# Attention beside a long convolution on one core: score tiles taken three in a row, probability products by halves of the queries

## The chip, the cores and the metric

The program runs on one core of one Trainium2 chip. The metric is device time in microseconds (us) of one execution: 1081.78 us is the median of three runs of the kernel before (1081.75 to 1082.9). A profiled execution of the same program is the source of every other number ahead of the prediction.

Four engines matter. TensorE (PE) does all matrix products and writes them to PSUM; a load of its stationary operand is shown apart as PEld. ScalarE (ACT) does almost nothing but the exponentials. VectorE (DVE) copies results out of PSUM and does the elementwise work. GpSimd (POOL) and SyncE (SP) mostly issue DMA transfers. Each engine runs its own instructions strictly in the order in which the program wrote them, and waits on semaphores for the others.

## The reference

Two independent results are computed and put side by side. Left, multi-query attention with 32 heads of width 16 and one shared key and value:

```python
q = (x @ wq).reshape(B, S, H, Dh)        # S = 2048, D = 512, H = 32, Dh = 16
k = x @ wk;  v = x @ wv                  # one head of keys and values for all
scores = einsum("bhqd,bkd->bhqk", q, k) * Dh ** -0.5
p = softmax(scores, axis=-1)
a = einsum("bhqk,bkd->bhqd", p, v).reshape(B, S, H * Dh) @ wo
```

Right, a gated long convolution per channel:

```python
k_shift = causal depthwise conv of k with 4 taps
kv = k_shift * v
y = causal conv of kv with ssm_k (length 2048, by FFT) + kv * ssm_D
b = q * y
out = concatenate([a, b], axis=-1)
```

## The kernel before, in words

**Attention, the main line.** The queries are cut into 32 blocks of four heads by 512 positions (`NQ` = 32), the keys into 16 tiles of 128 (`NKT` = 16). That gives 512 steps `i`, with n = i // 16 the query block and k = i % 16 the key tile. A step has two tiles of scores, so there are 1024 tiles `u`, two heads each. `scores(u)` puts two matmuls side by side in the upper and the lower half of the array (L673) into one of three PSUM tiles of two banks, and has ACT write exp of it (L681) into an SBUF tile `p` of 128 x 1024 floats, one of `PB` = 5. `pv(i)` multiplies the two `p` tiles of step i with the values (L690): four matmuls of 32 output columns, one for each head, side by side in the array, which add up over the 16 key tiles in one PSUM bank, `self.acc`. After the last key tile DVE copies that bank out (L700, tile `ao`) and DMA takes it to DRAM.

The order of the main line is written by hand in `attend`: in step i the score tiles 2i+4 and 2i+5, then `pv(i)`, then one call of `fill.step(i)`.

**Everything else is fill.** Query projections (`rest_of_q`), the normalization of finished heads (`wo_heads`), the output projection (`wo_part`), and the convolution by a two-stage Fourier transform (`conv_pe` for its matrix products and transposes, `conv_dve` for its elementwise stages) are Python generators. Each yields the price of its next piece, for PE and for DVE, before it writes it. `_Fill.step` adds `RATE` = 480 for PE and 1450 for DVE to two credits at each step and takes the next pieces from the generators in their order while the credit lasts, at most one piece with a PE price. The transposes of the convolution (`turn`, L248) and `bound`, one small matmul for each projection chunk (L555), have prices of their own. A piece of the helper `mm` (L191) is four matmuls side by side; a PE piece of price 920 is one `mm` of 512 columns or two of 256. HOLD keeps a PSUM bank with one generator over several steps. `finish` writes what is left of all generators ahead of the very last `pv`.

**PSUM.** Three score tiles take six banks. The other two (pool `pf`) serve `self.acc` and the fill: while the sum of a query block runs, one bank is left for the fill.

**The end.** `wo_part` has rows of `wo_rows` for head groups 12 and 13 (copied out at L786), then `over` (L818 to L824: transposes, reciprocal and product on DVE, for two halves of the last block but one), then eight products that are added to `wp` at L806 and L811; `last` does the last query block.

**Places of the text.** Lines here are those of the kernel before; the changed program numbers the same lines a little higher (scores L698, probability products L718, `mm` L196).

Of the kernel before, what the change touches and what calls it, by code (L numbers as in the profile page):

```python
# [19 lines left out]
P = 128  # L20
# [6 lines left out]
CB = 256  # L27
# [11 lines left out]
PB = 5  # L39


RATE = 480.0, 1450.0
MOST = 1400.0, 2900.0
SLACK = 60.0
OB = 5

Q_AT = 0, 40, 170, 295
# [37 lines left out]
class _Emit:  # L85
# [107 lines left out]
    def forward(self, src, c, m, ft):  # L193

        b = self.bank()
        for q in range(2):  # L196
            self.mm(b[:, q * CB : (q + 1) * CB], ft[:, q, :], src)
        self.nc.vector.tensor_copy(c[:, :, m, :], b.rearrange("p (q n) -> p q n", q=2))  # L198
# [36 lines left out]
    def long_forward(self, blk, hin, ch):  # L235
# [19 lines left out]
        for m in range(0, 16, 2):  # L255
            if m < 12:
                ft[m // 2 + 2] = self.table("ff", m // 2 + 2)
                yield 500, 700
                turn(m + 4)
            for i in range(2):  # L260
                yield 920, 700
                self.forward(hT[m][:, i, :], ch, m + i, ft[m // 2][:, i])
# [22 lines left out]
    def short_forward(self, blk, tpb, kk, cx):  # L285
# [3 lines left out]
        kv, ft = {}, {i: self.table("ff", i) for i in range(2)}  # L289

        def prod(m2):
# [3 lines left out]
            v = w.tile([P, 2, CB], F32, tag="s2", bufs=S2, name=self.nm("v"))  # L295
            nc.gpsimd.dma_start(v, self.vr[:, r, cs])
            if 2 <= m2 + 1 < 8:
                ft[m2 + 1] = self.table("ff", m2 + 1)
            a = w.tile([P, 2, CB], F32, tag="s2", bufs=S2, name=self.nm("a"))
# [4 lines left out]
            for i in (2, 1, 0):  # L304
                t = w.tile([P, 2, CB], F32, tag="s2", bufs=S2, name=self.nm("t"))
# [6 lines left out]
            kv[m2] = a  # L312

        yield WAIT, 3
        yield from prod(0)
        for m2 in range(8):
            if m2 < 7:
                yield from prod(m2 + 1)
            for i in range(2):
                yield 920, 700  # L320
                self.forward(kv[m2][:, i, :], cx, 2 * m2 + i, ft[m2][:, i])
# [16 lines left out]
    def backward(self, blk, cx, places):  # L338
# [15 lines left out]
        for m2 in range(8):  # L354
            if m2 < 6:
                load(m2 + 2)
            r = self.s2("r")
            for i in range(2):
                m = 2 * m2 + i
                yield 920, 450  # L360
                b = self.bank()
                for cc in range(2):
                    self.mm(
                        b[:, 0:CB],
# [5 lines left out]
                nc.vector.tensor_tensor(r[:, i, :], b[:, 0:CB], q[m2][:, i, :], ALU.mult)  # L370
# [5 lines left out]
    def conv_pe(self):  # L376

        yield from self.conv_load()
        self.sp = {}
        ld = self.short_load(0)  # L380
        yield WAIT, 5
        yield from self.short(0, ld)
# [6 lines left out]
        ld = self.short_load(1)  # L389
        yield from self.after(("y", 0))  # L390
        yield from self.backward(0, *self.sp["y", 0])
        yield from self.short(1, ld)
# [3 lines left out]
    def short(self, blk, loads):  # L396
        cx = self.spectrum()
        yield from self.short_forward(blk, *loads, cx)
        self.sp["cx", blk] = cx
        self.seen.add(("cx", blk))  # L400

# [132 lines left out]
    def q_mm(self, g, c, b, dk):  # L534
        self.mm(b, self.wq[g][:, dk, :], self.xT[c][:, dk, :], start=dk == 0, stop=dk == 3)
# [34 lines left out]
    def prologue(self):  # L570
# [5 lines left out]
        self.qa, self.st, self.pt = {}, {}, {}  # L576
# [42 lines left out]
        self.scores(3)  # L619

    def rest_of_q(self):
        for c, first in enumerate(Q_AT):
            while self.step < first:
                yield WAIT, 1
            for g in range(4):
                if c == g == 0:
                    continue
                if c or g > 1:
                    b = None
                    for dk in range(4):  # L630
                        yield (920, 0, HOLD) if dk < 3 else (920, 2600)
                        b = b or self.bank()
                        self.q_mm(g, c, b, dk)
# [5 lines left out]
            if c < 2:  # L639
                self.xT[c + 2] = self.w.tile([P, 4, 512], F32, tag="xt", bufs=2, name=f"xT{c + 2}")  # L640
                self.nc.sync.dma_start(self.xT[c + 2], self.xd[c])
        self.flag()

    def stack(self, n, rows=KR):

        c, h = n // 8, 4 * (n % 8)
        t = self.w.tile([P, 2, 512], F16, tag="st", bufs=3, name=self.nm("st"))
# [36 lines left out]
    def pv(self, i):  # L684
        nc, w = self.nc, self.w
        n, k = i // NKT, i % NKT
        if k == 0:
            self.acc = self.bank()
        for j in range(4):
            nc.tensor.matmul(  # L690
                self.acc[32 * j : 32 * j + 32, :],
                self.vx[:, k, :],
                self.pt[2 * i + j // 2][:, j % 2, :],
                start=k == 0,
                stop=k == NKT - 1,
            )
        if k < NKT - 1 or n == NQ - 1:
            return  # L698
        a = w.tile([P, 512], F32, tag="ao", bufs=2, name=self.nm("ao"))
# [6 lines left out]
    def attend(self, fill):  # L706
        self.od = self.dr.tile([NQ, P, 512], F32, name="od")
        for i in range(NQ * NKT):
            n, k = i // NKT, i % NKT
            self.step = i  # L710
            if k == 4 and 2 <= n + 1 < NQ:
                self.stack(n + 1)
            self.scores(2 * i + 4)
            self.scores(2 * i + 5)
            if i == NQ * NKT - 1:
                fill.finish()
            self.pv(i)
            fill.step(i)  # L718
# [42 lines left out]
    def wo_rows(self, i, groups):  # L761

        for G in groups:
            yield (920, 700) if G == groups[-1] else (920, 0, HOLD)
            if G == groups[0]:
                b = self.bank()
            self.mm(b, self.oc[G][:, i * P : (i + 1) * P], self.wo[G % 4], start=G == groups[0], stop=G == groups[-1])
# [80 lines left out]
class _Fill:  # L848
# [3 lines left out]
    def __init__(self, threads):  # L852
# [18 lines left out]
    def step(self, i):  # L871
# [3 lines left out]
        while more:  # L875
            more = False
            for t in self.threads:
# [3 lines left out]
                if a[0] > 0:  # L881
                    if c[0] < a[0] - SLACK or not once or self.holder not in (None, t):
# [14 lines left out]
    def finish(self):  # L897
        while any(t[0] is not None for t in self.threads):
            for t in self.threads:
                if t[0] is not None and next(t[0], None) is None:  # L900
                    t[0] = None
# [152 lines left out]
```

## Time and profile before

| | |
|---|---|
| median of the runs | 1081.78 us |
| the profiled execution, its own time | 1082.38 us |
| its span in the profile | 1080.5 us |
| granted TensorE clock over the span | 0.996 |
| PE busy | 1039.7 us, 96% |
| ACT busy | 976.5 us, 90%; 1024 exponentials |
| DVE busy | 612.1 us, 57% |
| POOL busy | 95.8 us, 9% |

A row of the page or of a group reads: line, engine, operation, output tile <- input tiles, shapes, xcount, then the busy time of the group and the mean of one in ns, then the idle time of the engine just ahead of the group and what ended it. A row of the timeline reads: start, length, engine, line, operation, xcount of instructions merged into the row, and in brackets the idle time before it with what ended it. Matmuls of four-byte floats are recorded as two instructions each, so a `pv` of four matmuls is a row of x8. Matmul records overlap; the distance between the starts of two rows is the better measure of what PE spends.

### The profile page before, as it was taken

Reading aid. Unit: us, or ns where it says so; the run is one execution under the profiler, and the core shown is the slowest. Engines: PE = TensorE matmul, PEld = TensorE weight load, DVE = VectorE, ACT = ScalarE, POOL = GpSimd, SP = SyncE. Lnnn points to the kernel's source line nnn. Section 1 sums busy time; section 2 is a strip of 40 time slices with the busy share of each in tenths; the row PEclk is TensorE's granted clock in tenths of the full one; section 3 lists DMA queues with packets and bytes.
Section 4 is the critical chain, followed back from the end, with each engine's and each line's share of the span. In section 5 each row is a group of like instructions: output and inputs, shape, how many; then the busy total and the mean of one; then the engine's idle time right before and its main releaser. Section 6 shows DMA issues by size and latency. Waiting matters only on the chain.

```text
span 1080.5 us, 21752 instructions
## 1 busy us (share of the span) xinstructions
PE 1039.7 (96%) x8947; PEld 261.3 (24%) x8947; DVE 612.1 (57%) x841; ACT 976.5 (90%) x1032; POOL 95.8 (9%) x149
## 2 busy tenths in 40 slices
PE   7899999999999999999999999999999999999995
PEld 4222222223322222233222222222221122222221
DVE  2547413766677767666767751355537876762123
ACT  2699999999999999999999999898999999999990
POOL 2032000100000000002202200011010000000210
PEclk9899999999999999999999999999999999999999
DMA  6455311331130111102314241132120111110411
GB/s 211 156 163 193 103 57 52 114 135 48 41 135 28 49 39 57 55 25 81 123 64 140 94 133 42 48 116 82 57 79 30 38 49 38 38 39 27 130 59 42
DMA packets 47510, 86.66 MB, mean 80 GB/s; under 512 B 11132, under 2 KB 26026, under 8 KB 46380
## 3 DMA queue, kind: packets, MB, share of 16 engines
q1 hardware_dynamic: 33996, 43.50, 12.4%
q0 software_dynamic: 11648, 40.89, 11.7%
q8 instruction: 72, 1.18, 0.4%
q10 hardware_dynamic: 1760, 0.81, 0.3%
q14 instruction: 34, 0.28, 0.1%
HBM read 60.16 MB, written 25.02 MB: 79 GB/s over the span
## 4 chain that ended last, share of the span: by engine, by line
PE 81%; ACT 8%; issue 5%; DVE 3%; DMA 2%; ACTq 0%; DVEq 0%
PE f L690 39%; PE s L673 21%; PE f L191 18%; ACT p L681 8%; PE f L248 1%; DMA msk<-in_msk 1%; DMA xc<-in_A_x 1%; PE f L476 0%; DVE gn L557 0%; DVE gm L568 0%; DVE kc L494 0%; DVE ao L700 0%; DMA qd<-qp 0%; PE f L555 0%; DVE wp L811 0%
## 5 line engine op out<-in xcount | busy, mean ns | idle before, releaser
L681 ACT ACTIVATE p<-s 128x1024 f32<-128x1024 f32 x1024 | 969.6, 1052 | 56.3 <-PE f L690 36.3
L690 PE MATMUL f<-p,vx 128*32 128x512 f32 x4096 | 546.4, 606 | 0.9 <-DVE ao L700 0.9
L673 PE MATMUL s<-st,kst 49*128 49x512 f16 x2048 | 330.0, 383 | 14.5 <-ACT p L681 2.3
L673 PEld LDWEIGHTS <-kst 49*128 49x128 f16 x2048 | 74.5, 94 | 418.9 <-issue 412.6
L690 PEld LDWEIGHTS f<-p,vx 128*32 128x32 f32 x4096 | 80.8, 108 | 191.4 <-issue 186.9
L129 DVE TENSOR_TENSOR sp<-sp 128x1024 f32<-128x1024 f32 x96 | 112.2, 1216 | 0.0
L198 DVE COPY sp<-f 128x512 f32<-128x512 f32 x64 | 44.2, 690 | 91.7 <-PE f L191 91.2
L541 DVE TENSOR_SCALAR cut<-f 128x512 f32<-128x512 f32 x16 | 11.1, 691 | 114.2 <-PE f L191 114.2
L191 PE MATMUL f<-xT,wq 128*32 128x512 f32 x512 | 66.3, 593 | 0.5 <-DVE gm L568 0.5
L191 PE MATMUL f<-wo,o 128*32 128x512 f32 x480 | 62.5, 593 | 2.4 <-DVE wp L806 2.4
L129 DVE TENSOR_TENSOR sp<-sp,sp 128x1024 f32<-128x1024 f32 x48 | 56.5, 1215 | 0.3
L700 DVE COPY ao<-f 128x512 f32<-128x512 f32 x31 | 21.3, 688 | 62.0 <-PE f L690 61.9
L370 DVE TENSOR_TENSOR r<-f,q 128x256 f32<-128x256 f32 x32 | 13.6, 424 | 60.5 <-PE f L191 60.4
L202 POOL DMA_DIRECT2D ff<-in_ff x32 | 17.6, 552 | 263.1 <-PE s L673 263.1
L778 DVE COPY wp<-f 128x512 f32<-128x512 f32 x12 | 8.3, 691 | 57.1 <-PE f L191 56.9
L371 POOL DMA_DIRECT2D out<-r x16 | 11.4, 714 | 305.4 <-DVE r L370 292.0
L191 PE MATMUL f<-a,ff 128*32 128x256 f32 x512 | 33.5, 379 | 1.3 <-DVE sp L198 1.3
L309 DVE TENSOR_TENSOR a<-a,t 128x512 f32<-128x512 f32 x48 | 33.2, 691 | 1.5
L191 PE MATMUL f<-sp,fi 128*32 128x256 f32 x512 | 33.5, 379 | 0.0
L191 PE MATMUL f<-hT,ff 128*32 128x256 f32 x512 | 33.5, 379 | 0.0
L307 DVE TENSOR_TENSOR t<-kk,tpb 128x512 f32<-128x512 f32 x48 | 32.8, 683 | 0.0
L191 PEld LDWEIGHTS f<-xT,wq 128*32 128x32 f32 x512 | 16.3, 110 | 37.7 <-issue 33.7
(106 smaller groups left out, 519.9 us busy)
## 6 DMA issues: line engine op xcount, KB each, us to landing
ff<-in_ff POOLq DMA_DIRECT2D x32, 256.0 KB, 4.3
od<-ao SPq DMA_DIRECT2D x30, 256.0 KB
kk<-in_B_k POOLq DMA_DIRECT2D x12, 640.0 KB, 4.8
qd<-qp SPq DMA_DIRECT2D x48, 128.0 KB
st<-qd SPq DMA_DIRECT2D x60, 98.0 KB
v<-in_B_v POOLq DMA_DIRECT2D x16, 256.0 KB, 4.5
hin<-in_B_ssm_k POOLq DMA_DIRECT2D x4, 1024.0 KB, 6.2
fi<-in_fi POOLq DMA_DIRECT2D x16, 256.0 KB, 3.5
```

Source lines behind the costliest of these rows:

```text
L129: v.tensor_tensor(part(out), part(a), part(b), op)
L191: self.nc.tensor.matmul(out[j : j + 32], w[:, j : j + 32], x, start=start, stop=stop)
L198: self.nc.vector.tensor_copy(c[:, :, m, :], b.rearrange("p (q n) -> p q n", q=2))
L202: self.nc.gpsimd.dma_start(t, self.I[n][:, 2 * m2 : 2 * m2 + 2])
L307: nc.vector.tensor_tensor(t, kx(i), tap(i), ALU.mult)
L309: nc.vector.tensor_tensor(a, a, t, ALU.add)
L370: nc.vector.tensor_tensor(r[:, i, :], b[:, 0:CB], q[m2][:, i, :], ALU.mult)
L371: nc.gpsimd.dma_start(self.orr[:, 2 * m2 : 2 * m2 + 2, D + blk * CB : D + (blk + 1) * CB], r)
L673: self.nc.tensor.matmul(s[:, e, :], self.kst[rows, k * P : (k + 1) * P], self.st[n][rows, pr, :], start=True, stop=True,)
L681: self.nc.scalar.activation(p, s, AF.Exp, scale=DH**-0.5 / SC / SC)
L690: nc.tensor.matmul(self.acc[32 * j : 32 * j + 32, :], self.vx[:, k, :], self.pt[2 * i + j // 2][:, j % 2, :], start=k == 0, stop=k == NKT - 1,
L700: nc.vector.tensor_copy(a, self.acc)
```

## The change

`attend` takes three score tiles u, u+1, u+2 in a row (u = 3, 6, 9, ...), then three halves of `pv`, then `fill.step`. A half x is 256 of the 512 query columns of step x // 2, again four matmuls side by side; the halves that follow the tiles u to u+2 are u-4, u-3 and u-2. Where a new query block begins inside such a group of three halves, `fill.step` is called ahead of that half and not at the end of the group. `RATE` is added once for each group, that is for one and a half steps. PE pieces of the fill are cut to half size (460); several may follow each other in one call if the same generator holds the bank. The `p` tiles are 6 instead of 5, the query tiles `st` 2 instead of 3, `ao` 1 instead of 2. The products of the short convolution have become a generator of their own (`conv_short`), two blocks ahead of the transform that uses them; the generators stand in another order, and `hurry` names one that goes first from a given step on. `finish` now keeps a held bank with its generator.

```diff
-PB = 5
+PB = 6
-RATE = 480.0, 1450.0
+RATE = 660.0, 2300.0
+WO_AT = 290, 370, 440
-Q_AT = 0, 40, 170, 295
+AHEAD = 2
+Q_AT = 0, 66, 194, 322
...
         for q in range(2):
+            yield (920 / 2, 700) if q else (920 / 2, 0, HOLD)
+            if not q:
+                b = self.bank()
             self.mm(b[:, q * CB : (q + 1) * CB], ft[:, q, :], src)
...
+    def hurry(self):
+
+        if self.qc < 4 and self.step >= Q_AT[self.qc]:
+            return 3
+        return 4 if any(self.step >= x and ("wo", 4 * c) not in self.seen for c, x in enumerate(WO_AT)) else None
...
-    def pv(self, i):
+    def pv(self, x):
+
         nc, w = self.nc, self.w
+        i, h = x // 2, x % 2
         n, k = i // NKT, i % NKT
-        if k == 0:
+        if k == h == 0:
             self.acc = self.bank()
+        cols = slice(256 * h, 256 * h + 256)
         for j in range(4):
             nc.tensor.matmul(
-                self.acc[32 * j : 32 * j + 32, :],
+                self.acc[32 * j : 32 * j + 32, cols],
                 self.vx[:, k, :],
-                self.pt[2 * i + j // 2][:, j % 2, :],
-                start=k == 0,
-                stop=k == NKT - 1,
+                self.pt[2 * i + j // 2][:, j % 2, cols],
+                start=k == h == 0,
+                stop=k == NKT - 1 and h == 1,
             )
...
-        for i in range(NQ * NKT):
-            n, k = i // NKT, i % NKT
-            self.step = i
-            if k == 4 and 2 <= n + 1 < NQ:
-                self.stack(n + 1)
-            self.scores(2 * i + 4)
-            self.scores(2 * i + 5)
-            if i == NQ * NKT - 1:
+        x, steps = 0, NQ * NKT
+        for u in range(3, 2 * steps + 3, 3):
+            for t in range(u, min(u + 3, 2 * steps)):
+                if t % 32 == 12 and 2 <= t // 32 + 1 < NQ:
+                    self.stack(t // 32 + 1)
+                self.scores(t)
+            self.step = x // 2
+
+            end = 2 * (min(u, 2 * steps) // 2) if u >= 2 * steps else min(x + 3, 2 * (u // 2))
+            if u >= 2 * steps:
                 fill.finish()
-            self.pv(i)
-            fill.step(i)
+
+            full = [y for y in range(x + 1, end) if y % (2 * NKT) == 0]
+            for y in range(x, end):
+                if y in full:
+                    fill.step(self.step)
+                self.pv(y)
+            if not full:
+                fill.step(self.step)
+            x = end
         self.last()
...
-                    if c[0] < a[0] - SLACK or not once or self.holder not in (None, t):
+                    if c[0] < a[0] - SLACK or not (once or self.holder is t) or self.holder not in (None, t):
...
-        threads = [em.rest_of_q(), em.wo_heads(), em.conv_pe(), em.wo_part(), em.conv_dve()]
-        em.attend(_Fill(threads))
+        threads = [em.wo_heads(), em.conv_pe(), em.conv_short(), em.rest_of_q(), em.wo_part(), em.conv_dve()]
+        em.attend(_Fill(threads, em.hurry))
```

Three places show how instructions move on PE. In the rows, `s` is a score tile, `kst` the keys as stationary operand, `p` a tile of probabilities, `vx` the values, and `f` a bank of pool `pf`; x2 is two equal rows. First, one step of the main line, before:

```order
L673 LDWEIGHTS kst
L673 MATMUL s_4136<-st_3696,kst 128x512
L673 LDWEIGHTS kst
L673 MATMUL s_4136<-st_3696,kst 128x512
L673 LDWEIGHTS kst
L673 MATMUL s_4141<-st_3696,kst 128x512
L673 LDWEIGHTS kst
L673 MATMUL s_4141<-st_3696,kst 128x512
L690 MATMUL f_3936<-p_4102,vx 32x512 x2
L690 MATMUL f_3936<-p_4107,vx 32x512 x2
L191 MATMUL f_4093<-xT_763,wq_87 32x512 x4
```

Of the changed program, the last tile of a group of three with the halves and the fill behind it (the two tiles ahead of it are the same rows with s_6056 and s_6061):

```order
L698 LDWEIGHTS kst
L698 MATMUL s_6066<-st_5709,kst 128x512
L698 LDWEIGHTS kst
L698 MATMUL s_6066<-st_5709,kst 128x512
L718 MATMUL f_6051<-p_5980,vx 32x256 x2
L718 MATMUL f_6051<-p_5985,vx 32x256 x2
L718 MATMUL f_6051<-p_6012,vx 32x256 x2
L718 MATMUL f_6051<-p_6017,vx 32x256 x2
L718 MATMUL f_6051<-p_6012,vx 32x256 x2
L718 MATMUL f_6051<-p_6017,vx 32x256 x2
L196 MATMUL f_6083<-hT_5846,ff_5537 32x256 x4
```

Six score matmuls stand where four stood, then the second half of one step and both halves of the next, then a fill piece of half size (x4 of 256).

Second, the place where a query block ends inside a group, on PE of the changed program (f_5641 is the sum of the old block, f_6051 that of the new one, f_6037 the fill):

```order
L718 MATMUL f_5641<-p_5938,vx 32x256 x2
L718 MATMUL f_5641<-p_5975,vx 32x256 x2
L718 MATMUL f_5641<-p_5938,vx 32x256 x2
L718 MATMUL f_5641<-p_5975,vx 32x256 x2
L196 MATMUL f_6037<-hT_5846,ff_5537 32x256 x8
L718 MATMUL f_6051<-p_5980,vx 32x256 x2
L718 MATMUL f_6051<-p_5985,vx 32x256 x2
L698 LDWEIGHTS kst
```

Before, two score tiles stood between the last product of a block and the first of the next one; here only the fill does. This form occurs 18 times.

Third, the end of the main line on PE, before (what `finish` writes stands between the last two steps' products):

```order
L690 MATMUL f_10304<-p_10526,vx 32x512 x2
L690 MATMUL f_10304<-p_10531,vx 32x512 x2
L690 MATMUL f_10304<-p_10550,vx 32x512 x2
L690 MATMUL f_10304<-p_10555,vx 32x512 x2
L191 MATMUL f_10590<-wo_376,o_9994 32x512 x4
L191 MATMUL f_10596<-wo_376,o_9994 32x512 x4
L191 MATMUL f_10602<-wo_376,o_9994 32x512 x4
L191 MATMUL f_10608<-wo_376,o_9994 32x512 x4
L191 MATMUL f_10614<-wl_9912,lr 32x512 x4
L191 MATMUL f_10620<-wl_9912,lr 32x512 x4
L191 MATMUL f_10626<-wl_9912,lr 32x512 x4
L191 MATMUL f_10632<-wl_9912,lr 32x512 x4
```

and in the changed program:

```order
L718 MATMUL f_12696<-p_12953,vx 32x256 x2
L718 MATMUL f_12696<-p_12958,vx 32x256 x2
L196 MATMUL f_12945<-wo_376,o_11185 32x256 x4
L196 MATMUL f_12945<-wo_378,o_11937 32x256 x4
L196 MATMUL f_13007<-wo_376,o_11185 32x256 x4
L196 MATMUL f_13007<-wo_378,o_11937 32x256 x4
L196 MATMUL f_13007<-wo_376,o_11185 32x256 x4
L196 MATMUL f_13007<-wo_378,o_11937 32x256 x4
L196 MATMUL f_13050<-wo_380,o_12378 32x256 x8
L196 MATMUL f_13060<-wo_380,o_12378 32x256 x8
L196 MATMUL f_13070<-wo_380,o_12378 32x256 x8
L196 MATMUL f_13080<-wo_380,o_12378 32x256 x8
```

The half of a row and the whole last row of head groups 12 and 13 (f_12945, f_13007) now stand here too, and with them on DVE both calls of `over` for the last block but one, which stood among the steps of the last block before; four products with `wl` follow, as before.

More of the change, by code (lines that the diff above doesn't have):

```diff
@@ L304, in prod @@
             for i in (2, 1, 0):
[L305 removed]
+                t = self.s2("t")
                 yield 0, 700
@@ L876, in step @@
             more = False
-            for t in self.threads:
+            first = self.hurry()
+            for t in sorted(self.threads, key=lambda t: t is not self.threads[first or 0]):
                 a = self.ask(t, i)
```

129 lines of the change are left out of this document (79 added, 50 removed).

## The prediction

> **What bounds the kernel now.** I read the page first, then the groups, then the timeline of single steps, then the chain and the waits (a row of the waits gives the total in us, the times, the longest).
>
> ```profile
> span 1080.5 us, 21752 instructions
> PE 1039.7 (96%) x8947; PEld 261.3 (24%) x8947; DVE 612.1 (57%) x841; ACT 976.5 (90%) x1032; POOL 95.8 (9%) x149
> PE 81%; ACT 8%; issue 5%; DVE 3%; DMA 2%; ACTq 0%; DVEq 0%
> L681 ACT ACTIVATE p<-s 128x1024 f32<-128x1024 f32 x1024 | 969.6, 1052 | 56.3 <-PE f L690 36.3
> ACT p L681 <- PE f L690: 36.3, 212, 0.9
> ACT p L681 <- PE s L673: 11.1, 38, 1.7
> ```
>
> PE is the bound by its busy time and by the chain, but ACT comes close behind, and its idle time has one main cause: 212 times an exponential had to wait for a `pv` that was still reading the `p` tile it wanted to overwrite. Both engines are tied by buffers, so one step has to be timed on both.
>
> ```profile
> 535.64 20.36 ACT L681 ACTIVATE p<-s 128x1024 f32<-128x1024 f32 x22 [0.16 <-PE f L690]
> 552.30 0.39 PE L673 MATMUL s<-st,kst 49*128 49x512 f16 x2
> 552.62 1.06 PE L690 MATMUL f<-p,vx 128*32 128x512 f32 x8
> ...
> 555.02 1.06 PE L690 MATMUL f<-p,vx 128*32 128x512 f32 x8
> 555.90 1.05 PE L191 MATMUL f<-sp,fi 128*32 128x256 f32 x16
> 556.17 1.02 ACT L681 ACTIVATE p<-s 128x1024 f32<-128x1024 f32 x1 [0.18 <-PE f L690]
> 556.88 0.61 PE L673 MATMUL s<-st,kst 49*128 49x512 f16 x4
> 557.37 1.02 ACT L681 ACTIVATE p<-s 128x1024 f32<-128x1024 f32 x1 [0.17 <-PE s L673]
> 557.41 1.07 PE L690 MATMUL f<-p,vx 128*32 128x512 f32 x8
> 558.41 0.60 PE L673 MATMUL s<-st,kst 49*128 49x512 f16 x4
> 558.95 1.06 PE L690 MATMUL f<-p,vx 128*32 128x512 f32 x8
> ```
>
> By starts: two score tiles to `pv` 0.54 (558.41 to 558.95), `pv` to scores 1.00, `pv` to fill 0.88, fill to scores 0.98. A bare step costs PE 1.54, one with a fill 2.40. One tile's scores take 0.39 and two 0.60 to 0.61, so a tile more is 0.22. ACT in its longest row without a wait: (20.36 - 1.02) / 21 = 0.92 from exponential to exponential, 1.02 for one alone (they overlap by 0.10). ACT's floor is 1024 x 0.92 = 942.
>
> Four delays across the engines: score start to exponential 0.49 (556.88 to 557.37); `pv` start to an exponential that waited for it 1.15 (555.02 to 556.17); a lone third tile to `pv` 0.32 (552.30 to 552.62); and the end of an exponential to the scores that wait for its PSUM tile:
>
> ```profile
> 551.03 1.22 ACT p L681
> 552.25 0.04 issue
> 552.30 0.39 PE s L673 x2
> ```
>
> about 0.05. The main line runs from tile 8, the second of this row, to tile 1022:
>
> ```profile
> 42.05 5.68 ACT L681 ACTIVATE p<-s 128x1024 f32<-128x1024 f32 x6 [0.34 <-PE f L690]
> 1050.47 1.02 ACT L681 ACTIVATE p<-s 128x1024 f32<-128x1024 f32 x1 [0.17 <-PE s L673]
> ```
>
> Tile 8 ends at 42.05 + 1.02 + 0.92 = 43.99, tile 1022 at 1051.49: 1007.5 us, the term that the change works on.
>
> **The change, part by part.** *Fewer turns.* A product of 256 columns has 379 ns a record, one of 512 has 593:
>
> ```profile
> L191 PE MATMUL f<-xT,wq 128*32 128x512 f32 x512 | 66.3, 593 | 0.5 <-DVE gm L568 0.5
> L191 PE MATMUL f<-a,ff 128*32 128x256 f32 x512 | 33.5, 379 | 1.3 <-DVE sp L198 1.3
> ```
>
> Two records each, so a half is 0.43 less. A group of three tiles and three halves costs PE 0.54 + 0.22 + 1.00 + 0.43 = 2.19 bare, against 1.5 x 1.54 = 2.31 now: 0.12 saved, 41 us over 341 groups. With one half piece of fill it is 0.76 + 1.31 + 0.55 = 2.62, with two 0.76 + 1.31 + 0.98 = 3.05 (1.31 is 0.88 + 0.43, 0.55 is 0.98 - 0.43). ACT needs 3 x 0.92 = 2.76 for a group.
>
> The halves themselves I cost at nothing: sixteen 256-column records go from 555.90 to the scores at 556.88, and eight of 512 take the same 0.98:
>
> ```profile
> 401.29 1.04 PE L191 MATMUL f<-xT,wq 128*32 128x512 f32 x8
> 402.27 0.61 PE L673 MATMUL s<-st,kst 49*128 49x512 f16 x4
> ```
>
> The Trainium skill's page "TensorE: Matmul & The Clock Gate" speaks against the halves: its section "Back-to-back issue gap" gives each matmul a fixed 2.5 ns beside its columns. By that an estimate is 12 more records a group, 30 ns, some 4 us over the groups with two pieces; the two rows above differ by eight records and by no time that they resolve.
>
> *The buffers.* This is where the gain goes. Scores of tile u+2 wait for the exponential of u-1 (three PSUM tiles), and all PE work behind them waits too: three halves, the fill and the next scores. So PE can't work ahead of ACT over a group. And the exponential of tile t overwrites the `p` tile of t-6. For an odd u the second exponential, u+1, needs the `p` tile of u-5, whose last reader is the first half behind the scores of the same group (half u-4). From the end of exponential u-1: 0.05 to the third score tile, 0.32 to the half, 1.15 - 0.43 = 0.72 to the exponential of u+1, then 0.92 and 1.02 to the end of u+2: **3.03** instead of 2.76, whatever the fill, up to two pieces. For an even u the readers are early enough, and 2.76 holds. A pair of groups takes at least 5.79.
>
> *Fill on top.* Two pieces in an odd group: next scores 0.05 + 0.32 + 1.31 + 0.98 = 2.66 after the exponential's end, its exponential at 3.15 where ACT was free at 3.03 - 0.10 = 2.93: 0.22 more, 6.01 a pair. Two pieces in an even group: the next group's third score tile comes at 2.66 + 0.44 = 3.10 and not at 2.76 + 0.05 = 2.81: 0.29 more, 6.08. The order of PE has 169 pairs of an odd and the following even group from tile 9 on. I count transposes and bounds as one piece:
>
> - at most one piece in either group: 48 x 5.79 = 277.9
> - two pieces in the odd group only: 48 x 6.01 = 288.5
> - two in the even group: 49 x 6.08 = 297.9
> - three in one: 6 x 6.5 = 39.0
> - with a block's end inside, as two in the even one: 18 x 6.08 = 109.4
>
> The sum is 1012.7 against 1007.5: **+5**.
>
> *The block's end inside a group*, 18 times. The new sum needs the bank of the old one copied out first:
>
> ```profile
> L700 DVE COPY ao<-f 128x512 f32<-128x512 f32 x31 | 21.3, 688 | 62.0 <-PE f L690 61.9
> PEld f L690 <- DVE ao L700: 2.6, 5, 1.1
> DVE ao L700 <- PE f L690: 61.9, 20, 12.3
> L129 DVE TENSOR_TENSOR sp<-sp 128x1024 f32<-128x1024 f32 x96 | 112.2, 1216 | 0.0
> ```
>
> So far PE lost 2.6 us to it, since scores lay between. Now: half to copy 0.72 (as to the exponential), copy 0.69, back 0.05, together 1.46; PE has 0.88 - 0.43 = 0.45 for the half and 0.88 for two fill pieces (11 places, 0.13 short) or 0.45 for one (7 places, 0.56 short): 5.3 us. DVE runs in order and is 57% busy, much of it with instructions of 1.22, so on average 0.57 x 0.61 = 0.35 more, 6.3 us: **+12**. From below 5; from above, where the DVE work that one call may write (2.3 less 0.7 for its copy, 1.6) lies ahead of each copy, 5.3 + 18 x 1.6 = 34. I take the middle value since 20 of 31 copies now find DVE waiting.
>
> *The end.*
>
> ```profile
> 1028.41 0.43 DVE L818 STREAM_TRANSPOSE lr<-ao 128x256 f32<-128x256 f32 x1
> 1032.21 0.42 DVE L824 TENSOR_TENSOR lr<-ao,lr 128x256 f32<-128x256 f32 x1
> 1050.52 1.92 PE L690 MATMUL f<-p,vx 128*32 128x512 f32 x16
> 1052.26 1.04 PE L191 MATMUL f<-wo,o 128*32 128x512 f32 x8
> 1053.37 0.69 DVE L806 TENSOR_TENSOR wp<-wp,f 128x512 f32<-128x512 f32 x1 [2.83 <-PE f L191]
> 1054.11 1.06 PE L191 MATMUL f<-wo,o 128*32 128x512 f32 x8 [0.81 <-DVE wp L806]
> 1066.28 1.04 PE L690 MATMUL f<-p,vx 128*32 128x512 f32 x8
> ```
>
> Here one bank is left for the fill, so products follow each other 1.86 apart (1052.26 to 1054.11), and the last `pv` starts 15.76 after the row at 1050.52. In the changed order, from the last three halves: 1.31 to the half row, 0.86 + 1.01 to the last row, 1.71 for it, 0.26 + 0.69 for its copy (0.26 is 1053.37 - 1052.26 - 0.85), then both `over`, 4.22 (1028.41 to 1032.63), which were hidden at 1028, and 0.69 + 0.05: 10.8. Six products at 1.86 and 0.88 for the seventh: 22.8, so 7.1 more. The three halves also start 0.2 ahead of the end of exponential 1022, and the row at 1050.52 started 1.0 ahead: **+8** in all; from below 4, if the `over` hide.
>
> *The start.* Tile 5 waits for the first of five `p` tiles, not for the first of six: about **-1**.
>
> ```profile
> 39.77 1.94 ACT L681 ACTIVATE p<-s 128x1024 f32<-128x1024 f32 x2 [0.79 <-PE f L690]
> ```
>
> The other edits (generator order, `hurry`, query tiles 2 for 3, `ao` 1 for 2) I cost at nothing: each query tile is asked for when its predecessor has long been read, and a projection chunk is written 27 groups or more ahead of its use. If that cover went, a transfer would show as a wait of scores.
>
> Sum: 5 + 12 + 8 - 1 = 24 on the profiled 1082.38, or 1106.4; the median lies 0.6 lower: **1106**.
>
> **The rivals.** *A: PE's order is all that counts.* The 41 us come in full and only the end costs 8: 1082 - 41 + 8 = 1049. For it: 96% and 81%. Against it: it asks ACT for 1007.5 - 41 = 966 over 1015 exponentials of 0.92, 934, with 32 left, while the odd groups' wait of 0.27 alone takes 46.
>
> *B: the slots bind, the fill doesn't.* If PE's slack in light groups carries over, 169.5 x 5.79 = 981, so 26 less, the end 8 more, the start 1 less, 1082 - 26 + 7 = 1063. For it: light and heavy groups alternate. Against it: the third score tile waits for an exponential in every group.
>
> *C: DVE late at every block's end,* the upper bound of that term: 34 for 12, 1128. It decides if the copy waits behind a whole call's DVE work. For it: the DVE credit rises from 1.5 x 1450 = 2175 to 2300 a group. Against it: the 20 of 31.
>
> **How the numbers follow.** The forecast (slots, fill on top, end) has 0.64, with a range of its own from 1083 (half of the fill's extra of 1012.7 - 981 = 32, and block ends at 5) to 1118 (block ends at 24, between the value taken and the upper bound). A has 0.12, B 0.12, C 0.12. The range from 1052 to 1127 leaves out most of A and half of C. A measurement can tell 0.2%, 2 us, from no change. Faster takes A, B and a little of the forecast's lower edge, 0.25; the same 0.03; slower 0.72.
>
> **What would show it.** Right: ACT's waits for `pv` near 170 of about 0.3 us, one in every second group, 50 us or more in all where 36.3 stood; PE's busy share well under 96%, with score rows waiting for ACT; new waits of PE for the `ao` copy, 18 of them or so; from the last exponential to the span's end 36 us instead of 28. Wrong: ACT's rows without a wait run over five groups and more (the slot chain is not there), or PE stays at 96% with a span under 1065 (A or B); the end as long as before.

## The result, and the profile after

The changed kernel takes 1112.66 us (median of four runs, 1111.45 to 1113.86) where the kernel before takes 1081.80: a ratio of 1.0283, interval 1.0265 to 1.0301. It is slower, by 31 us where 24 were forecast. The profiled execution took 1113.86 us. One of the ten runs of the kernel with two tiles a step, below, took 1177.56 us at a granted clock of 0.845 where its others had about 0.99; it counts in that kernel's median (1081.36 without it) and not in its ratio.

The page of the changed kernel, its totals, clock, chain and the group of the scores:

```profile
span 1112.1 us, 31796 instructions
PE 1031.5 (93%) x13971; PEld 464.8 (42%) x13971; DVE 609.3 (55%) x825; ACT 979.8 (88%) x1032; POOL 96.0 (9%) x149
PEclk9899999999999999999999999999999999999996
PE 62%; ACT 18%; issue 13%; DVE 5%; DMA 2%; POOL 0%; ACTq 0%; DVEq 0%; POOLq 0%
L698 PE MATMUL s<-st,kst 49*128 49x512 f16 x2048 | 318.2, 382 | 46.4 <-ACT p L706 43.9
```

PE's busy share fell from 96% to 93%, although it has the same arithmetic to do, and its share of the chain from 81% to 62%. What it lost is in the last row: the scores waited 43.9 us for exponentials. The clock is low in the second slice, where it is low in the kernel before too, and in the last. Neither engine is the bound any more; the buffers between them are. The waits say so from both sides (total in us, times, the longest). The kernel before has this row for the scores:

```profile
PE s L673 <- ACT p L681: 2.3, 10, 0.3
```

and the changed kernel these:

```profile
PE s L698 <- ACT p L706: 43.9, 155, 0.5
ACT p L706 <- PE s L698: 40.2, 86, 2.2
ACT p L706 <- PE f L718: 13.5, 66, 0.8
PEld f L718 <- DVE ao L728: 13.3, 18, 2.7
PE f L718 <- DVE ao L728: 5.3, 10, 2.2
DVE ao L728 <- PE f L718: 80.1, 22, 13.7
```

One stretch of the changed kernel without fill, as the timeline shows it, PE's rows first and then ACT's:

```profile
823.95 0.39 PE L698 MATMUL s<-st,kst 49*128 49x512 f16 x2 [0.53 <-ACT p L706]
824.27 1.50 PE L718 MATMUL f<-p,vx 128*32 128x256 f32 x24
825.70 0.77 PE L698 MATMUL s<-st,kst 49*128 49x512 f16 x4
826.99 0.39 PE L698 MATMUL s<-st,kst 49*128 49x512 f16 x2 [0.52 <-ACT p L706]
...
825.00 5.61 ACT L706 ACTIVATE p<-s 128x1024 f32<-128x1024 f32 x6 [0.18 <-PE f L718]
830.79 5.61 ACT L706 ACTIVATE p<-s 128x1024 f32<-128x1024 f32 x6 [0.18 <-PE f L718]
```

The third score tiles at 823.95 and 826.99 are 3.04 apart: the odd group of the slot chain, forecast at 3.03. ACT runs six exponentials and stops for a product with the probabilities, 5.79 after the last stop (825.00 to 830.79), the pair that was forecast. PE's turns for such a group add up to 2.19 by the prediction's sum; by starts, it stands idle for the rest.

The end of the changed kernel, PE's rows and the two of DVE that count:

```profile
1069.50 1.05 PE L196 MATMUL f<-wo,o 128*32 128x256 f32 x16
...
1073.97 0.43 DVE L863 STREAM_TRANSPOSE lr<-ao 128x256 f32<-128x256 f32 x1
1074.10 1.07 PE L196 MATMUL f<-wo,o 128*32 128x256 f32 x16 [0.81 <-DVE wp L831]
1077.77 0.43 DVE L869 TENSOR_TENSOR lr<-ao,lr 128x256 f32<-128x256 f32 x1
1078.85 1.89 PE L196 MATMUL f<-wo,o 128*32 128x256 f32 x16 [3.67 <-DVE wp L851]
1081.53 1.93 PE L196 MATMUL f<-wo,o 128*32 128x256 f32 x16 [0.79 <-DVE wp L851]
...
1095.28 1.93 PE L196 MATMUL f<-wl,lr 128*32 128x512 f32 x8 [0.81 <-DVE wp L856]
1096.99 1.93 PE L718 MATMUL f<-p,vx 128*32 128x256 f32 x16
```

Both `over` (1073.97 to 1078.20) now lie open, as forecast, and PE stands 3.67 us in front of the row that needs a bank behind them. What was not forecast comes next: from 1078.85 the products follow each other 2.7 apart and take 1.9, where the same rows at 1069.50 and 1074.10 take 1.06. The windows of the same execution (PE, PEld, DVE, ACT and POOL busy with their counts, then granted clock, DMA share, GB/s) name the cause:

```profile
1064.00:1079.00 15.00, 9.45 (x151) 4.30 (x144) 5.78 (x15) 5.37 (x6) 0.00 (x0) 1.00 0.01 1
1079.00:1099.00 20.00, 15.13 (x100) 3.63 (x97) 4.83 (x8) 0.00 (x0) 0.00 (x0) 0.50 0.00 1
```

The clock was halved for 20 us (in the trace's record of the clock from 1078.96 for 20.48 us), from the moment at which PE took up work again. Seven products and the two last halves of the products with the probabilities (the row at 1096.99) ran in that time, and the products stood some 0.88 further apart than at full clock: about 6 us.

Where the 31 us went, against the profiled execution before. All terms are between fixed points: the end of tile 8 at 42.29 (43.99 before), the end of tile 1022 at 1068.4, the span's end.

| term | forecast | measured |
|---|---|---|
| start, to the end of tile 8 | -1 | -1.7 |
| main line, tile 8 to tile 1022 | +5 and +12 | 1026.1 - 1007.5 = +18.6 |
| end, from tile 1022 on | +8 | 43.7 - 29.0 = +14.7 |
| own time of the profiled execution | +24 | +31.5 |

(The sum of the three is 31.6; the time outside the span is 0.1 shorter.)

### The profile page after: what moved, and what is told of

The parts are those of the page before. It is cut to its first block, busy times and chain, and to the rows that moved or that the text cites. A ratio compares the mean times of both kernels' runs of the same rounds, so it can differ in the third digit from the quotient of the medians.

```text
span 1112.1 us, 31796 instructions
## 1 busy us (share of the span) xinstructions
PE 1031.5 (93%) x13971; PEld 464.8 (42%) x13971; DVE 609.3 (55%) x825; ACT 979.8 (88%) x1032; POOL 96.0 (9%) x149
## 4 chain that ended last, share of the span: by engine, by line
PE 62%; ACT 18%; issue 13%; DVE 5%; DMA 2%; POOL 0%; ACTq 0%; DVEq 0%; POOLq 0%
PE f L718 30%; ACT p L706 18%; PE s L698 17%; PE f L196 13%; PE f L255 1%; DVE sp L134 1%; DMA wkv<-in_A_wk 1%; DVE ao L728 1%; DMA xc<-in_A_x 0%; DMA ff<-in_ff 0%; PE x L479 0%; PE f L496 0%; DVE kc L514 0%; DVE sp L205 0%; DVE cut L561 0%
## 5 line engine op out<-in xcount | busy, mean ns | idle before, releaser
L706 ACT ACTIVATE p<-s 128x1024 f32<-128x1024 f32 x1024 | 972.8, 1030 | 71.1 <-PE s L698 40.2
L718 PE MATMUL f<-p,vx 128*32 128x256 f32 x8192 | 521.2, 386 | 5.3 <-DVE ao L728 5.3
L698 PE MATMUL s<-st,kst 49*128 49x512 f16 x2048 | 318.2, 382 | 46.4 <-ACT p L706 43.9
L718 PEld LDWEIGHTS f<-p,vx 128*32 128x32 f32 x8192 | 230.9, 110 | 224.3 <-issue 97.8
L698 PEld LDWEIGHTS <-kst 49*128 49x128 f16 x2048 | 98.1, 94 | 286.0 <-issue 237.4
L196 PE MATMUL f<-wo,o 128*32 128x256 f32 x960 | 68.9, 392 | 6.9 <-DVE wp L851 5.3
L196 PE MATMUL f<-xT,wq 128*32 128x256 f32 (+1 forms) x960 | 69.9, 394 | 0.0
L561 DVE TENSOR_SCALAR cut<-f 128x512 f32<-128x512 f32 x16 | 11.1, 691 | 98.4 <-PE f L196 98.4
L381 DVE TENSOR_TENSOR r<-f,q 128x512 f32<-128x512 f32 x16 | 11.1, 691 | 74.0 <-PE f L196 74.0
L196 PEld LDWEIGHTS f<-wo,o 128*32 128x32 f32 x960 | 31.2, 112 | 30.7 <-DVE wp L851 7.5
L196 PEld LDWEIGHTS f<-xT,wq 128*32 128x32 f32 x960 | 31.1, 110 | 21.9 <-issue 2.1
L196 PE MATMUL f<-a,ff 128*32 128x256 f32 x512 | 36.3, 387 | 0.8 <-DMA ff<-in_ff 0.6
```

What stands on the lines that cost most here:

```text
L196: self.nc.tensor.matmul(out[j : j + 32], w[:, j : j + 32], x, start=start, stop=stop)
L381: nc.vector.tensor_tensor(r, b.rearrange("p (i n) -> p i n", i=2), q[m2], ALU.mult)
L698: self.nc.tensor.matmul(s[:, e, :], self.kst[rows, k * P : (k + 1) * P], self.st[n][rows, pr, :], start=True, stop=True,)
L706: self.nc.scalar.activation(p, s, AF.Exp, scale=DH**-0.5 / SC / SC)
L718: nc.tensor.matmul(self.acc[32 * j : 32 * j + 32, cols], self.vx[:, k, :], self.pt[2 * i + j // 2][:, j % 2, cols], start=k == h == 0, sto ...
```

## The experiments

**One `p` tile more.** If the odd group's wait for the slot of tile u-5 is the chain, a seventh `p` tile removes it, with PE's order unchanged. The tile count of `S2` makes room in SBUF.

```diff
-S2 = 7
-PB = 6
+S2 = 5
+PB = 7
```

> The changed kernel with 7 tiles of probabilities instead of 6 (the memory comes from the convolution's small tiles, 5 instead of 7). Slot theory: the second exponential of an odd group finds its tile free, so pairs of groups without fill fall from 5.79 to 5.52 us, odd groups from at least 3.04 to 2.76, and the time falls by about 48 x 0.27 + 49 x 0.07 = 16 to 17 us to some 1096; the end is as long as before. Rival (the slots only carry a wait that PE's order sets anyway): odd groups stay at 3.04 and the time at 1112 or more.

1095.41 us, a ratio of 1.012 (1.010 to 1.014): 17 us of the 31 are gone, and the profile of this kernel has lost the pattern. ACT's row and PE's third score tiles in the same stretch:

```profile
814.30 22.16 ACT L706 ACTIVATE p<-s 128x1024 f32<-128x1024 f32 x24
822.76 0.39 PE L698 MATMUL s<-st,kst 49*128 49x512 f16 x2 [0.39 <-ACT p L706]
825.51 0.39 PE L698 MATMUL s<-st,kst 49*128 49x512 f16 x2 [0.39 <-ACT p L706]
```

Every group of this stretch now takes 2.75, a pair 5.50 where it took 5.79, and ACT runs 24 exponentials without a wait, 0.92 apart. The main line from the end of tile 8 to that of tile 1023 falls from 1027.1 to 1009.8; the end stays (43.0 after 42.7). The slot chain is shown. But 1009.8 is still no better than the 1008.7 before: with the slots out of the way the groups with at most one piece of fill stand at ACT's 3 x 0.92 (median 2.75 from the end of a group's last exponential to that of the next), those with two pieces take 3.18, and PE, whose third score tile waits for an exponential, can't use what its order saves.

**`over` earlier.** The end is tested by itself: the two `over` leave `wo_part` for a generator of their own, so that DVE does them ahead of the rows of head groups 12 and 13.

```diff
     def wo_part(self):
...
-        both = w.tile([P, 2, 3, 512], F32, tag="in", bufs=1, name="lr")
-        t, self.lr = both[:, 0], both[:, 1]
-        while self.step < 16 * (NQ - 1) + 1:
-            yield WAIT, 1
-        for h in range(2):
-            yield 0, 1800
-            self.over(self.ao, t, h)
+        yield from self.after(("lr", 0))
+        t = self.lt
...
+    def wo_over(self):
+        while self.step < 16 * (NQ - 1) + 1:
+            yield WAIT, 1
+        both = self.w.tile([P, 2, 3, 512], F32, tag="in", bufs=1, name="lr")
+        self.lt, self.lr = both[:, 0], both[:, 1]
+        for h in range(2):
+            yield 0, 1800
+            self.over(self.ao, self.lt, h)
+        self.seen.add(("lr", 0))
```

> The changed kernel with the two divisions of the last block but one (over) in a generator of their own, so that they stand ahead of the last rows of head groups 12 and 13 on VectorE. Theory: 4.2 us of VectorE work leave the end, TensorE no longer stands still for 3.7 us there, and its granted clock stays at 1.0, so the seven products after it fall from 2.7 to 1.86 apart; from the end of tile 1022's exponential to the span's end 33 to 34 us instead of 43.7, the time about 1102. Rival (the clock falls because the last products wait for one bank, whatever stands ahead): the end loses only 4, the clock still falls to half, 1108.

1103.01 us, 1.0181 (1.0164 to 1.0197): 9.7 us less than the changed kernel. The window over the products of the end, and three of their rows:

```profile
1068.00:1088.00 20.00, 12.67 (x172) 4.56 (x168) 6.88 (x10) 0.09 (x1) 0.00 (x0) 1.00 0.00 1
1074.71 1.07 PE L196 MATMUL f<-wo,o 128*32 128x256 f32 x16 [0.81 <-DVE wp L846]
1076.59 1.07 PE L196 MATMUL f<-wo,o 128*32 128x256 f32 x16 [0.81 <-DVE wp L846]
...
1086.01 1.07 PE L196 MATMUL f<-wl,lr 128*32 128x512 f32 x8 [0.81 <-DVE wp L851]
```

No half clock over the products (the clock's record has it from 1096.77 on only, behind them), the products 1.88 apart, the end from tile 1022 on 34.3 where it was 43.7; the main line is untouched (1027.3 to the end of tile 1023). The wait in front of the row at 1078.85 was 3.67 - 0.81 = 2.9 longer than the others; the rest of the 9.4, 6.5, is the clock. This shows that the half clock hangs on the wait that is taken away here; that the clock and not the wait alone slowed the rows is in the rows' own lengths, 1.07 against 1.93. The two other kernels of this study in which the wait of 3.67 us stands at this place have the half clock behind it too: 20.48 us with seven `p` tiles, 23.89 us in the next experiment.

**The third tile between the blocks.** Where a query block ends inside a group, its last half is written ahead of the third score tile, so that these scores cover the copy of the old sum.

```diff
+            split = u < 2 * steps - 3 and any(y % (2 * NKT) == 0 for y in range(x + 1, min(x + 3, 2 * (u // 2))))
             for t in range(u, min(u + 3, 2 * steps)):
+                if split and t == u + 2:
+                    while True:
+                        self.pv(x)
+                        x += 1
+                        if x % (2 * NKT) == 0:
+                            break
...
-            full = [y for y in range(x + 1, end) if y % (2 * NKT) == 0]
+            full = [x] if split else []
```

> The changed kernel with the third score tile moved between the old block's last half and the new block's first half, at the 20 groups in which a block ends. Theory: the copy of the old sum gets about 0.6 us more cover, TensorE's waits for it fall from 18.6 us to under 8, the time by 6 to 10 us to about 1104. Rival (VectorE comes to the copy late, whatever TensorE does): the waits stay over 12 us and the time within 3 us of 1112.

1109.84 us, 1.0250 (1.0233 to 1.0268). The time is the rival's, within 3 us of 1112; the waits lie between the two expectations. PE's waits for the copy in this kernel:

```profile
PEld f L718 <- DVE ao L728: 7.1, 11, 2.2
PE f L718 <- DVE ao L728: 2.3, 2, 1.9
```

The two rows together fell from 18.6 to 9.4, but the main line only by 3.0 (1024.1 where it was 1027.1). The sum of the two rows is no price. One block's end in the changed kernel shows why:

```profile
199.88 0.16 PEld L718 LDWEIGHTS f<-p,vx 128*32 128x32 f32 x8 [0.89 <-DVE ao L728]
199.88 0.64 PE L718 MATMUL f<-p,vx 128*32 128x256 f32 x8 [0.41 <-DVE ao L728]
```

This is one wait in two rows, and the loads of the stationary operand also stand idle while earlier matmuls still run. The matmuls' own row fell from 5.3 to 2.3, by the same 3.0 as the main line. So TensorE's matmuls stood still for 5.3 us at the ends of blocks and not for 18.6, and the 6 to 10 us expected were read from the wrong row. Each such group also has one turn more between products and scores now; what that cost was not separated.

**Halves without rows of three.** The old main line of two score tiles a step, with everything else of the change left in: halves, half pieces of fill, six `p` tiles, the new generators.

```diff
-RATE = 660.0, 2300.0
+RATE = 440.0, 1533.0
...
+        self.scores(3)
...
+        for i in range(steps):
+            self.scores(2 * i + 4)
+            self.scores(2 * i + 5)
+            self.pv(2 * i)
+            self.pv(2 * i + 1)
+            fill.step(i)
```

> The changed kernel with the old main line: two score tiles, then both halves of a step, then one call of the fill with two thirds of the credits for a group. All else (half pieces, halves of the product, six tiles of probabilities, the generators and their order) stays. Theory (the three in a row are what costs): TensorE bounds again, 403 steps with one half piece at 1.54 + 0.43 = 1.97, 67 bare ones at 1.84 by ScalarE, 40 others near 2.0: about 991 us from tile 8 to 1022 against 1007.5 before and 1026 in the change; with an end like the one before about 1065, with the changed one's up to 1080. Rival (the halves and the other edits cost the time): 1095 or more, and steps with one half piece well over 1.97.

1081.51 us, 0.9982 (0.9972 to 0.9992): the loss is gone, so all of it belongs to the rows of three with their buffers and end. But the 991 us expected of the main line did not come: tile 8 to tile 1022 took 1007.1. The timeline of one step with half a piece of fill, in this kernel:

```profile
400.32 0.60 PE L699 MATMUL s<-st,kst 49*128 49x512 f16 x4
400.86 1.07 PE L719 MATMUL f<-p,vx 128*32 128x256 f32 x16
401.74 0.61 PE L196 MATMUL f<-xT,wq 128*32 128x256 f32 x8
402.29 0.60 PE L699 MATMUL s<-st,kst 49*128 49x512 f16 x4
```

400.32 to 402.29 is 1.97 = 1.54 + 0.43, and 1.97 is also the median of all 404 steps with half a piece: halves cost nothing, and half a piece costs half a piece. The expectation left out single steps that take longer. At the ends of blocks PE has two rows of waits for the copy:

```profile
PEld f L719 <- DVE ao L729: 18.5, 29, 2.4
PE f L719 <- DVE ao L729: 5.9, 6, 1.9
```

The row of the weight loads, 2.6 us in the kernel before, is not what PE lost. Here are the weight loads of the last products of one block and of the first ones of the next:

```profile
449.60 0.59 PEld L719 LDWEIGHTS f<-p,vx 128*32 128x32 f32 x16 [0.42 <-issue]
...
451.57 0.59 PEld L719 LDWEIGHTS f<-p,vx 128*32 128x32 f32 x16 [0.42 <-DVE ao L729]
```

The wait of 0.42 stands in both, the second time under another name, and the step takes its 1.97. At another block's end PE did lose time:

```profile
164.28 0.68 DVE L312 TENSOR_TENSOR t<-kk,tpb 128x512 f32<-128x512 f32 x1
164.88 0.68 DVE L729 COPY ao<-f 128x512 f32<-128x512 f32 x1
165.62 1.07 PE L719 MATMUL f<-p,vx 128*32 128x256 f32 x16 [1.43 <-DVE ao L729]
```

The last products with the probabilities had started at 162.14, and DVE had an instruction of the convolution ahead of the copy until 164.88. That is the mechanism of rival C, found in another kernel, at five of the 31 block ends: there the copy started 0.4 to 2.1 us after the products' end (0.07 at the others), and the five steps took 6.0 us more than 1.97 each. Five other steps took 9.0 us more together: one waited 2.7 us for a transfer of `ff`, one 1.1 us for DVE, and in four of the five, that of the transfer among them, the clock stood at half (three dips of 3.41 us in the clock's record, from 548.45, 633.78 and 708.88). The bare steps came out about as much below the expectation as the remaining ones above it.

**The kernel before with six `p` tiles.** Is the `p` tile worth something without the rest? In the kernel before, with `st` and `ao` smaller by one as in the change.

```diff
-PB = 5
+PB = 6
...
-        t = self.w.tile([P, 2, 512], F16, tag="st", bufs=3, name=self.nm("st"))
+        t = self.w.tile([P, 2, 512], F16, tag="st", bufs=2, name=self.nm("st"))
...
-        a = w.tile([P, 512], F32, tag="ao", bufs=2, name=self.nm("ao"))
+        a = w.tile([P, 512], F32, tag="ao", bufs=1, name=self.nm("ao"))
```

> The kernel before with the change's buffers alone: 6 tiles of probabilities instead of 5, 2 query tiles instead of 3, 1 copy tile instead of 2. Theory: with two tiles a step TensorE's order binds, so the 36 us that ScalarE waited for probability tiles only move to other waits: 1082, within 3 us. Rival (the tiles of probabilities bind the old order too): ScalarE gains most of the 36 us, 1060 or less.

1078.80 us, 0.9966 (0.9954 to 0.9978), 3.8 us less. In the waits of this kernel the row of 36.3 us for the products with the probabilities is gone, and the row for the scores has grown from 11.1:

```profile
ACT p L681 <- PE s L673: 50.2, 207, 2.0
```

36.3 us of waits are gone and 39.1 are there under another name, since PE's order sets the pace in that kernel (82% of the chain): the main line fell by 4.0, from 1008.7 to 1004.7 to the end of tile 1023.

**The repairs together.** Seven `p` tiles, the early `over`, and one thing more: the last eight products go, two and two added up in one bank, into banks of the score tiles, which are free by then, and no longer one after the other through the one bank that is left. (`ending` is set with the last group, ahead of `finish`; the early `over` and the seventh tile are as above.)

```diff
-        for i in range(4):
-            b = yield from self.wo_rows(i, range(14, 15))
-            nc.vector.tensor_tensor(self.wp[i], self.wp[i], b, ALU.add)
...
+        while not self.ending:
+            yield WAIT, 1
+        s = [self.wide() for _ in range(2)]
+        for i in range(4):
+            yield 1840, 700
+            b = s[i // 2][:, i % 2, :]
...
+            self.mm(b, t[:, 2, i * P : (i + 1) * P], self.wl[0], start=False)
+            nc.vector.tensor_tensor(self.wp[i], self.wp[i], b, ALU.add)
```

> Three tiles in a row with the two repairs together (7 tiles of probabilities; the divisions early) and with the last eight products of head group 14 and of wl in the banks of the score tiles, two added up in one bank, so that none waits for VectorE. Theory: the repairs add up, 1112 - 17 - 10 = 1085, and the end loses another 6 to 7 for the eight products: 1078 to 1079. Rival (the repairs overlap): 1085 or more.

1081.15 us, 0.9990 (0.9978 to 1.0002). Main line 1010.9 to the end of tile 1023, end 27.0 behind it: both repairs hold side by side, 2 us short of what was expected. With the new waits and the long end repaired, rows of three tiles come out where the kernel started. The 41 us of turns that they save on PE never arrive.

**The same end in the other two kernels.** The edit on the last eight products alone, in the kernel before and in the kernel of two tiles and halves:

> The kernel before with only the last eight products moved to the banks of the score tiles. Theory: eight products at 0.86 in place of 1.86 apart, 14.0 us of them become 7, and the main line is untouched: 1075, 0.6% faster than before. Rival (the last products hide behind something else, or the score banks are free too late): 1080 or more.

> The changed kernel with two tiles a step again, as in the run before, and with the last eight products in the banks of the score tiles. Theory: 1081.5 less 6 to 7, 1075. Rival: 1080 or more.

1077.19 us, 0.9954 (0.9941 to 0.9968), and 1073.99 us, 0.9920 (0.9906 to 0.9933). With the same end, rows of three (1081.15) stay 7 us behind two tiles a step (1073.99). The kernel before is 5 us better where 7 were expected, and its timeline shows why:

```profile
1052.69 1.04 PE L192 MATMUL x<-wl,lr 128*32 128x512 f32 x8
1054.54 1.07 PE L192 MATMUL x<-wo,o 128*32 128x512 f32 x8 [0.81 <-DVE wp L814]
...
1059.00 1.06 PE L192 MATMUL x<-wo,o 128*32 128x512 f32 x8 [0.81 <-DVE wp L814]
```

The third and the seventh product wait 0.81 each for an addition on DVE, though they write another bank than the one it reads: it is the other bank of the same tile. In the trace the weight load ahead of the third product waits for a semaphore of VectorE, and starts (1054.54) when the addition has ended (1054.49): the program itself contains this wait. So the banks were taken in turns:

```diff
-        for i in range(4):
+        for i in (0, 2, 1, 3):
```

> The kernel of the run before (two tiles a step, last eight products in score banks), with the four banks taken in turns of the two tiles, 0, 2, 1, 3. Theory: the products of a second bank waited for VectorE since it still read the first bank of the same tile (two waits of 0.81 and a pitch of 1.86 there); with turns the waits go and the end loses another 1 to 2 us: 1072 to 1073. Rival (they wait for the score tile to be free, not for VectorE): 1074, unchanged.

1072.05 us, 0.9901 (0.9885 to 0.9918). The waits are gone; the first of the eight products and the row behind the last one in the timeline of this kernel:

```profile
1048.37 1.04 PE L197 MATMUL x<-wo,o 128*32 128x512 f32 x8
...
1055.24 1.05 PE L720 MATMUL f<-p,vx 128*32 128x256 f32 x16
```

Eight products take 8 x 0.86 (1048.37 to 1055.24), and the end behind tile 1023 is 20.7 us, 27.8 in the kernel before. This is the best version of the study, about 10.8 us ahead of the kernel before and some 40 ahead of the change.

## Why the prediction was right, and where it was wrong

The direction, the size (1106 of 1112.7) and the main cause hold.

*The slot chain* holds to a hundredth. Forecast: 3.03 for an odd group, 5.79 for a pair, whatever the fill up to two pieces. Measured: 3.04 and 5.79, and with one more `p` tile 2.75 and 5.50. The ladder of pairs, forecast and median measured (from the end of the last exponential of an odd group to that of the next odd one): at most one piece 5.79 and 5.79, two in the odd group 6.01 and 6.02, two in the even one 6.08 and 6.09, three in one 6.5 and 6.52. The fill stands on top of the slots as the sum had it, and rival B, in which light groups would carry it, falls by that. Rival A falls by the 93% and 62%, and by the seventh `p` tile: even without the slot chain the lighter groups stand at ACT's 2.75, since scores can't run ahead of three PSUM tiles, and those with two pieces at 3.18.

*The block ends* were costed at 12 for 18 groups, and came out a little cheaper: pairs with a block's end took 6.56 in the mean where 6.08 + 12/18 = 6.74 was in the sum. DVE was mostly free for the copy, 22 of 31 times by the waits; in some of the others it came late, at the most by 1.6 us. Rival C, DVE late everywhere, is not what happened here. The mean rests on two of the 18: they took 9.38 and 7.58, and a half clock of 3.41 us (from 331.4 and 720.6) falls into each; the other 16 took 6.20 to 6.64, 6.32 in the mean. At those 16 the ends of blocks cost 3.8 us over 6.08 where the sum has 10.7, so that the whole term came as near as 8.7 is partly luck. The prediction also took the row of the weight loads (2.6) for what PE had lost before; the matmuls' row has 0.9 there and 5.3 in the changed kernel. Main line in all: 17 forecast, 18.6 measured, as the means of the other pairs lie some hundredths over the values used.

*The failed step is the end*, +8 in the sum, +14.7 measured. Its mechanism was right (both `over` open, seven products in a row through one bank) and its size was worked out at full clock: from the three last halves to the last half row 10.8 + 6 x 1.86 + 0.88 = 22.8. In the trace it is 1068.18 to 1096.99, 28.8, and the 6 us are the half clock that followed on the open `over`. The prediction priced the idle time of PE as idle time alone. The Trainium skill's page "TensorE: Matmul & The Clock Gate", in its section "Why this matters for your kernels", advises to leave no gap of more than about 3 us between bursts of matmuls, or the clock gate falls back to half speed. The trace agrees for this gap: 3.67 us without a matmul, then 0.50. But shorter gaps, of 2.16 and 1.84 us, were followed by 0.50 in the same trace (last section).

*What would show it.* Claimed were 170 waits of ACT for products with the probabilities, 50 us and more. There were 66, 13.5 us. The loss was there but not under that name: of the 0.29 that a bare pair loses (5.79 for 5.50), ACT's record shows 0.18 as a wait, and 0.10 is the overlap of two exponentials that a wait destroys, which counts as busy; and where fill lies in the pair, the scores arrive still later than the slot, so that the wait is recorded for them (86 times, 40.2 us). The other signs came as claimed: 93%, 18 waits of weight loads for the copy, a longer end (from the end of the last exponential 42.7, where 36 was claimed).

*After the prediction* the weakest expectation was that of halves without rows of three: 991 us of main line, 1007.1 measured. It took PE's undisturbed steps as the bound. Of the 16 us, 6.0 are five late copies at block ends, which the prediction had priced for the change itself, and 9.0 are five steps with another wait or the half clock in them.

## What to carry to other kernels

Count, for each tile that is overwritten, how many instructions lie between its last reader and its next writer in the order of the engine that reads it; writing work in longer rows saves turns on one engine and takes away exactly this distance, and here one more buffer tile was worth 17 us where 41 us of saved turns were worth nothing. A wait shown for one engine can come back in full under the name of the next releaser, so what a removed wait is worth is read from the engine that sets the pace, and there from the distance between its instructions: the waits of weight loads added up to 18.5 us in a kernel whose matmuls waited 5.9. At the end of a kernel, ask of each stretch that loses its cover what it does to the clock as well as to the order, and look for buffers that have just become free.

## What the runs showed of the hardware

Not expected: the length of the half clock. After one gap of 3.67 us PE ran at 0.50 for 20.48 us, although it was busy 15.13 of the first 20 and its gaps were only 0.8 long; the rows of its products took 1.93 for 1.06. The same gap of 3.67 us in two more kernels was followed by 20.48 and 23.89 us of half clock, while without it the same products kept the full clock with the same short gaps, though PE was busy for only 12.67 us of 20. Shorter gaps can be followed by shorter dips: the clock's record of the changed kernel also has 0.5 for 3.41 us from 331.4 and from 720.6, each less than 1.4 us after the start of one of these rows.

```profile
330.71 1.28 PE L718 MATMUL f<-p,vx 128*32 128x256 f32 x16 [2.16 <-DVE ao L728]
...
719.23 0.27 PE L685 MATMUL f<-ident,g 128*1 128x128 f32 x1 [1.84 <-DVE g L683]
```

The same gap of 1.84 us, at the same instruction, had no dip behind it in the kernels with seven `p` tiles and with the early `over`, so its length alone does not decide. Why the long one lasted six times as long as these was not tried.

The second surprise is in the two-bank tiles: matmuls into one bank waited 0.81 for VectorE's reading of the other bank of the same tile, and did not when the banks were taken alternately from two tiles. The wait is a semaphore of the program, which the addition on VectorE ends; whether the hardware would have needed it, no run here tells.
